# Two layers of attention and MLP on one core: VectorE's share of the exponentials gets a tile of its own, a new gate, and new numbers in the planner

## The chip, the cores and the metric

The kernel runs on one core of one Trainium2 chip. The core has five engines that run side by side: TensorE (PE in the profile) for matmuls, VectorE (DVE), ScalarE (ACT), GpSimd (POOL) and SyncE (SP), which issues the DMAs. Each engine takes its instructions in the order in which the program wrote them and waits on semaphores for the others. The metric is the time of one execution on the device in microseconds.

## What is computed

`x` is 2048 rows of 448. It goes twice through attention and a squared-ReLU MLP, with the same weights both times:

```python
x = x + _A_ref(_layernorm(x), A_wqkv, A_wo)
x = x + _B_ref(_layernorm(x), B_w1, B_b1, B_w2, B_b2)
x = x + _A_ref(_layernorm(x), A_wqkv, A_wo)
x = x + _B_ref(_layernorm(x), B_w1, B_b1, B_w2, B_b2)
```

In `_A_ref` there are 16 heads of width 28, and each head takes the softmax of a 2048 x 2048 matrix of scores. In `_B_ref` the hidden width is 1792: `h = x @ w1 + b1`, then `relu(h)` squared, then `@ w2 + b2`. The exponentials are the bulk of the elementwise work: 2 layers x 16 heads x 2048 x 2048 values, which is 2048 units of 128 x 512.

## The kernel before

**Units and groups.** The scores are cut into units of 128 keys-rows x 512 columns (one head, two blocks of 128 keys, 256 queries). `s_stream` (L746) takes three units at a time, a group: the score matmuls (L810) write three banks of a PSUM tile `sc`, of which there are two. `e_stream` (L826) then has ScalarE take the exponential of the whole group in one instruction (L835), from `sc` into a bfloat16 tile `pt`. There are 11 `pt` tiles. `p_stream` (L934) multiplies the exponentials with V (L984) and adds up `oT`.

**VectorE's units.** When `apart` (L704) says yes, the third unit of a group is not given to ScalarE: ScalarE's instruction is then 1024 columns wide, and VectorE computes the third exponential with five instructions (`a_unit` L880, `a_rest` L899). It takes the scores from PSUM and turns them into integers, `i` (L891); from the upper half of each integer it makes a power of two, `e` (L905); it multiplies a first factor into `e` (L911); it makes a second factor from the lower half, `f`, and writes it over `i` (L917); and it multiplies the two into a bfloat16 tile (L924). `f` is the lower half of `i`, so L917 writes what L911 has to have read. There are two sets of scratch tiles, `R_v`: `v_i` and `v_e`, and for most of the run a second pair that lies in a part of `K_sb` that is not in use.

**When `apart` says yes.** A set must be free, a place for the result must be free, the keys and queries must be there, the group number must be at least `LEAD` = 20, and there must be at least `STOP` = 90 units to come. Then comes a gate on VectorE's load: `pl.load(SPAN, "DVE")` is the share of the last 14 us in which VectorE was busy by the planner's reckoning. If it is above `BUSY` = 0.95 the answer is no; and if the MLP work of the layer is behind a straight line through `LINES` (`behind`, L689), the bound is `LOW` = 0.8.

**The planner.** There is no run-time scheduler. `Planner.run` (L172) simulates the engines while the program is being written: every `Op` carries an engine, a duration and what it depends on. At each step it takes, of the next operations of all streams, the one that can start first, and where two can start at the same time the one whose stream has the lower number. The order so found is the order of the instructions in each engine's queue, and nothing changes it later. For VectorE the planner lets the next operation start 0.08 us before the end of the one in front (`OVER`), and lets an operation that depends on another one of VectorE start no earlier than 0.03 us after its end. The streams' numbers are 0 for scores, 1 for ScalarE's exponentials, 2 for `p_stream`, `C_PRIO` = 1.5 for L891, `EV` = 3.5 for evictions of PSUM tiles, 4 to 4.8 for the MLP chains of the blocks (`chain`, L1118), and for the other four instructions of a VectorE unit `V_PRIO` = 7, falling to `V_LATE` = 3.6 when the unit has waited for 5.5 us and to `V_LAST` = 1.8 when it is 8 groups old.

**The rest of VectorE's work.** It evicts the projections (L572, L576, L604), the transposes (L506), the ReLU and its square (L1162, L1169), the sums into `x_sb` (L1115) and `oT` (L1007, L1009); and it takes the row moments for the layer norms: `stats` (L444) is one planner operation of 0.74 us that writes two instructions one behind the other, L449 (the moments of a row) and L450 (their mean and variance), of which the second needs the first. GpSimd makes the reciprocal root (L471, L472), and L521 applies it.

**Fill.** TensorE's score matmuls are repeated up to three times where it would sit idle, and `heat` (L1205) adds matmuls whose result nobody reads (L1220).

Of the kernel before, what the change touches and what calls it, by code (L numbers as in the profile page):

```python
# [11 lines left out]
DT = mybir.dt  # L12
# [26 lines left out]
LINES = ((280, 1312, 7.6), (1440, 2040, 6.6))  # L39
MARGIN = 2.0  # L40
LOW = 0.8
TURNS = 1
# [11 lines left out]
WINDOW = 2.8  # L54
C_PRIO = 1.5
V_PRIO = 7.0
V_LATE = 3.6
V_LAST = 1.8
V_AGE = 8
V_PAST = 3  # L60
OWN3 = 0
FIRST = 90
V_FIRST = 9.2
V_WAIT = 5.5
NEAR = 9
FAR = 15
KEEP = 3
LAG = 5
LEAD = 20
LAST = 690  # L70
BUSY = 0.95
SPAN = 14.0
NPT = 11
# [9 lines left out]
HOLD1 = 7  # L83
SOON = 0.6
NHP = 3
THIRD = 1
NL = 0
NLP = 3.8
STOP = 90
HSTOP = 0  # L90
CHUNK = 2
EV = 3.5
CUTS = (0, 10, 16)
# [124 lines left out]
def kernel(  # L218
# [225 lines left out]
    def stats(mv, t0, j, deps):  # L444
        def fn(e):
            st = sp.tile([P, 6], DT.float32, name="st")
            if mv[0] is None:
                mv[0] = sp.tile([P, 4, 2], DT.float32, name="mv")
            nc.vector.bn_stats(out=st[:, :], in_=x_sb[:, t0 + j, :])  # L449
            nc.vector.bn_aggr(out=mv[0][:, j, :], in_=st[:, :])  # L450
        o = Op("DVE", 0.74, fn, deps=deps)
        mv[1].append(o)
        return o

    def layernorm(t0, nt, deps_of, early=False, mv=None, place=None):


        if mv is None:
            mv = moments()
            for j in range(nt):  # L460
                yield stats(mv, t0, j, deps_of(j))
        ln = {}
# [23 lines left out]
        def turn(p0, own, xs):  # L486
            box = {}

            def tr(e, xs=xs):
                tp = bank(t, "tp").bitcast(DT.bfloat16).rearrange("p (c q) -> p c q", c=NDC)  # L490
                box["t"] = tp
                for k, (xn, _) in enumerate(xs):
                    for dc in range(NDC):
                        nc.tensor.transpose(out=tp[:, dc, k * P:(k + 1) * P],  # L494
                                            in_=xn[:, dc * P:(dc + 1) * P], identity=ident[:, :])
            t = Op("PE", 0.07 * NDC * len(xs), tr, deps=[x[1] for x in xs],
                   acq=pools_now(early) if early else spare(1))
            yield t

            def ev(e, p0=p0, w=len(xs) * P):  # L500
                tp = box["t"]
                dst = xnT[:, :, p0 * P:p0 * P + w]
                if e == "ACT":
                    nc.scalar.copy(out=dst, in_=tp[:, :, 0:w])
                else:
                    nc.vector.tensor_copy(out=dst, in_=tp[:, :, 0:w])  # L506
            o = Op("DVE", 0.12 + 0.3 * len(xs), ev, deps=[t], rel=t, sets=[("xT", t0 + p0)] if early else ())
            ends.append(o)
            pl.spawn(EV, iter([o, Op("DVE", 0.0, None, deps=[t], rel=own)]))

        wide = 1 if single else 2
        for p0 in range(0, nt, wide):
            js = range(p0, min(p0 + wide, nt))
            own = Op("DVE", 0.0, None, acq=R_xn)
            yield own
            xs = []
            for j in js:
                xn = xns[2 * (own.turn % 2) + j % 2]

                def norm(e, j=j, xn=xn):  # L520
                    nc.vector.tensor_scalar(out=xn[:, 0:D], in0=x_sb[:, t0 + j, :],  # L521
                                            scalar1=mv[0][:, j, 0:1], scalar2=ln[j],
                                            op0=ALU.subtract, op1=ALU.mult)
                nm = Op("DVE", 0.42, norm, deps=[rss[j]], sets=[("n", t0, j)] if early else ())
                yield nm
                xs.append((xn, nm))

            todo.append((p0, own, xs))
            if early and p0 + wide < nt:
                continue  # L530
            while todo:
                p0, own, xs = todo.pop(0)
                yield from turn(p0, own, xs)
        return xnT, own_xt, ends

    def mm_tile(subs, evac, ev_dur, deps, any_engine=False, sets=(), early=False, post=(), acq=None, alone=0):
# [25 lines left out]
        e = Op(engs_now(early) if any_engine else ("DVE",), ev_dur, lambda e: evac(e, box["t"]), deps=[last], rel=first, acq=acq, sets=sets)  # L562
        pl.spawn(EV, iter([e, *[p(e) for p in post]]))
        return e
# [14 lines left out]
    def qkv(l, t0, nt, xnT, own_xt, ends, early=False):  # L579
# [4 lines left out]
        def turned(w, dst, key, wkey, g0, r=r):  # L584
# [4 lines left out]
                 for i, g in enumerate(range(g0, g0 + r))],  # L589
                copy_to(d, q_scale if key == "Q" else None), 0.14 + 0.00109 * r * n, [*ends, *[(wkey, g) for g in range(g0, g0 + r)]], True,  # L590
                [(key, l, g, tb) for g in range(g0, g0 + r) for tb in range(t0, t0 + nt)], early and (t0 or g0 == 0))
# [97 lines left out]
    def behind(i):  # L689
# [3 lines left out]
        return done[l] < (min(i, b) - a) / (b - a) * n * per[l] - MARGIN  # L693
    pending = [0]

    def sets_of(unit):
# [7 lines left out]
    def apart(i, now, us, soon=SOON):  # L704
# [20 lines left out]
        if any(pl.tok.get(d) is None or pl.tok[d].end + LAT["DVE"] > now for d in needs(units[j])):  # L725
            return None
        if pl.load(SPAN, "DVE") > (LOW if behind(i) else BUSY):
            return None
        return j
# [96 lines left out]
    def e_stream():  # L826
        gi = 0
        while gi < len(gbuf) or s_left:
# [3 lines left out]
            def fn(e, gi=gi, n=n):  # L832
# [4 lines left out]
                if gbuf[gi].get("x") is gbuf[gi]["s"]:  # L837
                    apart_from(gi, t)
            o = gbuf[gi]["e"] = Op("ACT", n / 1200 + 0.05, fn, deps=[("s", gi)], acq=R_pt, need=n // 512,
                                   rel=gbuf[gi]["s"], sets=("e", gi))  # L840
# [25 lines left out]
    v_i = const.tile([P, 512], DT.int32, name="v_i")  # L866
    v_e = const.tile([P, 512], DT.int32, name="v_e")

    def set_of(res, l):

        k = R_v.index(res)
        two = lambda a: a.rearrange("p (a n) -> p a n", a=2)
        if k == 0:
            i, e = two(v_i[:, :]), two(v_e[:, :])
        else:
            keys = K_sb[1 - l][:, :, S - 512:S] if l == 0 else K_sb[0][:, :, 0:512]
            i, e = keys[:, 0:2, :].bitcast(DT.int32), keys[:, 2:4, :].bitcast(DT.int32)
        return i, e, two

    def a_unit(gi, x, src, unit, l):  # L880
# [3 lines left out]
        def take(e):  # L884
            pending[0] -= 1
            box["i"], box["e"], two = set_of(c.res, l)
            box["two"] = two
# [5 lines left out]
            if x is gbuf[gi]["s"]:  # L893
                apart_from(gi, t)
        c = Op("DVE", 0.69, take, deps=[("s", gi)], acq=sets_of(unit), rel=x)
        yield c
        pl.spawn(lambda now: V_LAST if e_now[1] - gi >= V_AGE or at[0] > ends_at[unit[0]] + V_PAST else V_LATE if now > c.end + V_WAIT else V_PRIO if gi > FIRST else V_FIRST, a_rest(gi, c, box, unit))

    def a_rest(gi, c, box, unit):  # L899
# [7 lines left out]
        p = Op("DVE", 0.42, power, deps=[c])  # L907
        yield p

        def first(e):  # L910
            nc.vector.scalar_tensor_tensor(out=flt("e"), in0=box["f"], scalar=root, in1=flt("e"),  # L911
                                           op0=ALU.add, op1=ALU.mult)
        g = Op("DVE", 0.68, first, deps=[p])
        yield g

        def square(e):
            nc.vector.scalar_tensor_tensor(out=flt("i"), in0=box["f"], scalar=lin, in1=box["f"],  # L917
                                           op0=ALU.add, op1=ALU.mult)
        h = Op("DVE", 0.68, square, deps=[c])
        yield h  # L920

        def close(e):
            pd = gbuf[gi]["pd"] = pd_of(o)
            nc.vector.scalar_tensor_tensor(out=box["two"](pd), in0=flt("i"), scalar=low, in1=flt("e"),  # L924
                                           op0=ALU.add, op1=ALU.mult)
        o = Op("DVE", 0.68, close, deps=[g, h], acq=lambda: pd_free(unit), rel=c, sets=("x", gi))
        gbuf[gi]["x"] = o
        yield o

    norm_done = {}  # L930
# [108 lines left out]
    def norm_stream(l, qb, g, res, oe, pair):  # L1039
# [13 lines left out]
        def rcp(e):  # L1053
            box["r"] = rp.tile([P, 2, QR], DT.float32, name="rec")[:, 0, :]
            nc.vector.reciprocal(out=box["r"][:, 0:n], in_=box["t"][:, 0:n])  # L1055
        r = Op("DVE", n * 0.0066, rcp, deps=[d], rel=d, acq=R_rec)
        yield r
# [12 lines left out]
    def norm_pair(l, qb, g, pair):  # L1070
# [15 lines left out]
        def rcp(e):  # L1086
            nc.vector.reciprocal(out=box["d"][:, :, 0:w], in_=box["d"][:, :, 0:w])
        r1 = Op("DVE", 0.33, rcp, deps=[d1])
        yield r1
# [28 lines left out]
    def chain(l, qb):  # L1118
# [10 lines left out]
        for j in range(nt):  # L1129
            a = yield from mm_tile(  # L1130
                [(0, D, [(oTn[:, g, j * P:(j + 1) * P], wo[:, g, :], *([("on", l, qb, g)] if end else [])) for g in range(G)])],
                add_to_x(t0 + j), 0.62, [*([] if end else norm_done[l, qb]), *[("wo", i) for i in range(G)]],
                post=[lambda a, j=j: stats(mv, t0, j, [a])], alone=G - 1 if end else 0)
# [18 lines left out]
        for f0 in range(0, NFC, pack):  # L1152
# [18 lines left out]
            def then(o, b=b, square=square):  # L1171
                aside = not s_left and (l, qb) == (1, len(blocks[1]) - 2)
                b["s"] = Op("ACT" if aside else "DVE", 0.5 if aside else 0.42, square, deps=[o], rel=o)
                return b["s"]
            o = yield from mm_tile(
                [(i * n, n, [(w1[:, dc, fc * P:(fc + 1) * P], xnT[:, dc, 0:n]) for dc in range(NDC)])
                 for i, fc in enumerate(fcs)],
                relu, 0.70, [*ends, ("w1",)], True, post=[then], acq=R_r)
            done[l] += w / 512
# [4 lines left out]
        for j in range(nt):  # L1184
# [3 lines left out]
            for lo, hi in halves:  # L1188
                def store(e, tb=tb, lo=lo, hi=hi):
# [5 lines left out]
                    post=[(lambda a, j=j: stats(mv, t0, j, [a])) if l == 0 else  # L1195
                          (lambda a, store=store: Op("DMA", 0.5, store, deps=[a]))])
            done[l] += 2.8
# [73 lines left out]
```

## Time and profile before

Three runs took 881.72, 882.03 and 882.49 us; the median is 882.03. The profiled execution has a span of 880.3 us, so 1.7 us lie around the span.

| | busy us | share of the span | instructions |
|---|---|---|---|
| ScalarE | 865.8 | 98% | 704 |
| of it the exponentials (L835) | 852.0 | 97% | 683 |
| TensorE | 825.4 | 94% | 12786 |
| VectorE | 795.1 | 90% | 1567 |
| GpSimd | 39.2 | 4% | 98 |

Of the 683 exponentials, 528 are 1536 columns wide and 155 are 1024 wide; VectorE has 154 units (528 x 3 + 155 x 2 + 154 = 2048). A row of the groups is to be read as: line, engine, operation, what it writes and reads, count, busy time and mean duration in ns, and the idle time of the engine just before. A row of the waits reads: who waited, for whom, us in total, how often, the longest. Instructions of one engine can overlap, so durations may add up to more than busy time.

### The profile page before, as it was taken

The page shows a single profiled execution, that of the slowest core. Times are in us where ns is not written, and L with a number is a line of the kernel's source. Part 1 is how long each engine was busy: PE and PEld are TensorE (multiplying, and loading weights), DVE is VectorE, ACT ScalarE, POOL GpSimd, SP SyncE. Part 2 cuts the span into 40 slices and gives each one's busy share as a digit, 9 for nine tenths or more (in the row PEclk, how much of TensorE's full clock was granted, in tenths as well). Part 3 has the DMA queues.
Part 4 walks back from the last instruction along what each step waited for, and adds up shares of the span by engine and source line. Part 5 has one row for each costly group of instructions (what it writes and reads, how often), then busy time and mean ns, then how long its engine had stood idle before and what let it go on. Part 6 is the DMA issues. An engine that isn't in the chain of part 4 may idle for free.

```text
span 880.3 us, 29041 instructions
## 1 busy us (share of the span) xinstructions
PE 825.4 (94%) x12786; PEld 452.0 (51%) x12786; DVE 795.1 (90%) x1567; ACT 865.8 (98%) x704; POOL 39.2 (4%) x98
## 2 busy tenths in 40 slices
PE   9999999999999999999999999899999999999998
PEld 5455554544545445455554545444545454445566
DVE  7998999999999899999989999999989899999854
ACT  8999999999999999999999999999999999999995
POOL 3100000001010000100001000000000000000000
PEclk9999999999999999999999999999999999999999
DMA  9100100000000000000000000110000000000100
GB/s 260 45 3 1 28 15 15 14 15 16 14 3 14 14 15 15 11 6 15 1 2 2 1 2 2 28 28 27 24 9 20 25 20 20 19 7 15 32 20 13
DMA packets 33914, 18.43 MB, mean 21 GB/s; under 512 B 18874, under 2 KB 33339, under 8 KB 33788
## 3 DMA queue, kind: packets, MB, share of 16 engines
q1 hardware_dynamic: 33788, 16.58, 6.8%
q8 instruction: 100, 1.64, 0.7%
q14 instruction: 26, 0.21, 0.1%
HBM read 14.26 MB, written 2.07 MB: 19 GB/s over the span
## 4 chain that ended last, share of the span: by engine, by line
ACT 77%; issue 12%; PE 10%; DVE 0%; ACTq 0%
ACT pt L835 77%; PE mt L554 4%; PE sc L810 3%; PE oT L984 2%; PE sc L554 1%; PE mt L330 1%; PE tp L494 0%; PE mt L1220 0%; DVE rec L1055 0%; PE den L1049 0%; DVE xnT L506 0%; ACT r L1160 0%; DVE oTn L1060 0%; DVE x_sb L1115 0%; DVE b2w L312 0%
## 5 line engine op out<-in xcount | busy, mean ns | idle before, releaser
L835 ACT ACTIVATE pt<-sc 128x1536 bf16<-128x1536 f32 (+1 forms) x683 | 852.0, 1527 | 1.2 <-PE sc L810 1.2
L810 PE MATMUL sc<-Q_sb,K_sb 32*128 32x256 bf16 (+1 forms) x5806 | 321.1, 265 | 45.3 <-ACT pt L835 39.9
L810 PEld LDWEIGHTS <-K_sb 32*128 32x128 bf16 x5806 | 151.2, 92 | 223.6 <-issue 191.5
L984 PE MATMUL oT<-pt,V_sb 128*32 128x256 bf16 (+1 forms) x4034 | 151.9, 268 | 0.0
L554 PE MATMUL mt<-xnT,w 128*128 128x256 bf16 (+1 forms) x912 | 119.8, 270 | 1.8 <-DVE xnT L506 0.6
L984 PEld LDWEIGHTS <-V_sb 128*32 128x32 bf16 x4352 | 91.0, 96 | 46.1 <-issue 43.1
L554 PEld LDWEIGHTS <-w 128*128 128x128 bf16 x952 | 78.7, 98 | 36.9 <-issue 28.9
L1162 DVE TENSOR_SCALAR r<-mt 128x512 bf16<-128x512 f32 x106 | 72.3, 682 | 8.2 <-PE mt L554 7.3
L554 PE MATMUL mt<-w,V_sb 128*128 128x448 bf16 (+2 forms) x288 | 67.9, 346 | 0.0
L891 DVE TENSOR_SCALAR v_i<-sc 128x512 int32<-128x512 f32 x87 | 59.5, 684 | 9.0 <-PE sc L810 8.6
L917 DVE SCALAR_TENSOR_TENSOR v_i<-v_i 128x512 f32<-128x512 uint16 x87 | 59.4, 683 | 1.3
L911 DVE SCALAR_TENSOR_TENSOR v_e<-v_i,v_e 128x512 f32<-128x512 uint16 x87 | 59.4, 683 | 0.8
L891 DVE TENSOR_SCALAR K_sb<-sc 128x512 int32<-128x512 f32 x67 | 45.8, 683 | 9.1 <-PE sc L810 9.0
L917 DVE SCALAR_TENSOR_TENSOR K_sb<-K_sb 128x512 f32<-128x512 uint16 x67 | 46.0, 687 | 1.3
L471 POOL TENSOR_TENSOR ve<-mv,eps_t 128x2 f32<-128x2 f32 (+1 forms) x34 | 9.5, 279 | 827.2 <-DVE mv L450 827.2
L911 DVE SCALAR_TENSOR_TENSOR K_sb<-K_sb 128x512 f32<-128x512 uint16 x67 | 45.8, 684 | 0.4
L1220 PE MATMUL mt<-xn,ident 128*128 128x448 bf16 x127 | 44.3, 356 | 1.6 <-DVE xn L521 0.6
L1115 DVE TENSOR_TENSOR x_sb<-x_sb,mt 128x448 bf16<-128x448 bf16 (+2 forms) x63 | 37.8, 601 | 7.5 <-PE mt L554 7.3
L449 DVE BATCH_NORM_STATS2 st<-x_sb 128x6 f32<-128x448 bf16 x64 | 39.7, 620 | 1.1 <-DMA x_sb<-in_A_x_dram 0.6
L554 PEld LDWEIGHTS <-V_sb 128*128 128x128 bf16 x302 | 24.9, 97 | 24.6 <-issue 10.1
L905 DVE TENSOR_SCALAR v_e<-v_i 128x512 int32<-128x512 int16 x87 | 36.4, 418 | 0.4
L984 PE MATMUL oT<-V_sb,V_sb 128*32 128x256 bf16 (+1 forms) x182 | 32.4, 273 | 0.0
(102 smaller groups left out, 792.1 us busy)
## 6 DMA issues: line engine op xcount, KB each, us to landing
rec<-scr SPq DMA_DIRECT2D x56, 128.0 KB
x_sb<-in_A_x_dram SPq DMA_DIRECT2D x8, 224.0 KB
out_dram<-x_sb SPq DMA_DIRECT2D x15, 112.0 KB
w<-in_B_w_dram SPq DMA_DIRECT2D x1, 1568.0 KB
w<-in_B_w_dram SPq DMA_DIRECT2D x1, 1344.0 KB
dn<-oT_sb SPq DMA_DIRECT2D x56, 4.0 KB
V_sb<-in_A_wqkv_dram SPq DMA_DIRECT2D x4, 168.0 KB
scr<-dn SPq DMA_DIRECT2D x28, 8.0 KB
```

The source lines that it names most:

```text
L449: nc.vector.bn_stats(out=st[:, :], in_=x_sb[:, t0 + j, :])
L554: nc.tensor.matmul(box["t"][:, c0:c0 + n], lhsT=lhsT() if callable(lhsT) else lhsT, rhs=rhs, start=a, stop=b)
L810: nc.tensor.matmul(dst[k][:, i * nt * P:(i + 1) * nt * P], lhsT=K_sb[l][rows, g, (kb + i) * P:(kb + i + 1) * P], rhs=Q_sb[rows, g, t0 * P: ...
L835: t = nc.scalar.activation(out=pt[:, 0:n], in_=gbuf[gi]["sc"][:, 0:n], func=AF.Exp, scale=float(np.log(2.0)) * 2.0 ** -FRAC)
L891: t = nc.vector.tensor_scalar(out=box["i"], in0=two(src), scalar1=EXP_BIAS, scalar2=EXP_LOW, op0=ALU.add, op1=ALU.max)
L905: nc.vector.tensor_scalar(out=box["e"], in0=box["n"], scalar1=2.0 ** 22, scalar2=EXP_BASE, op0=ALU.mult, op1=ALU.add)
L911: nc.vector.scalar_tensor_tensor(out=flt("e"), in0=box["f"], scalar=root, in1=flt("e"), op0=ALU.add, op1=ALU.mult)
L917: nc.vector.scalar_tensor_tensor(out=flt("i"), in0=box["f"], scalar=lin, in1=box["f"], op0=ALU.add, op1=ALU.mult)
L984: nc.tensor.matmul(box["t"][DHP * hh:DHP * hh + DHP, 0:n], lhsT=V_sb[l][:, kb + i, 4 * g + hh, :], rhs=p[:, c0:c0 + n], start=begin and kb ...
L1115: nc.vector.tensor_tensor(out=x_sb[:, tb, lo:hi], in0=x_sb[:, tb, lo:hi], in1=t[:, 0:hi - lo], op=ALU.add)
L1162: nc.vector.tensor_scalar(out=r[:, 0:w], in0=t[:, 0:w], scalar1=0.0, scalar2=None, op0=ALU.max)
L1220: nc.tensor.matmul(t[:, 0:D], lhsT=ident[:, :], rhs=xns[0][:, 0:D], start=True, stop=True)
```

## The change

Five things are changed together.

1. A scratch tile `v_h` is added. For the set `v_i`/`v_e` the second factor (L917) goes into `v_h` and not over `i`; it depends on L891 alone and is put in front of L911. For the set in `K_sb` the second factor still goes over `i`; it now depends on L911 in the planner's eyes too.
2. `stats` becomes two planner operations, 0.62 us and 0.182 us, so that another instruction may come between them.
3. Many durations in the planner are replaced; an exponential of n columns is n/1200 + 0.066 us where it was n/1200 + 0.05.
4. `apart` has a new gate: VectorE's open work, that is how far its clock is ahead plus what is left of the units begun (2.74 us for one just begun), must not be above `TB` = 4.8 us, or above `TB2` = 1.2 us when the MLP is behind. The load gate stays, over 8 us and not 14, with `BUSY` = 1.1 and `LOW` = 0.9.
5. The streams' numbers and other constants are changed.

```diff
-MARGIN = 2.0
-LOW = 0.8
+MARGIN = 1.5
+LOW = 0.9
...
-C_PRIO = 1.5
-V_PRIO = 7.0
-V_LATE = 3.6
-V_LAST = 1.8
+C_PRIO = 2.3
+V_PRIO = 8.5
+V_LATE = 5
+V_LAST = 2.7
 V_AGE = 8
-V_PAST = 3
+V_PAST = 4
 OWN3 = 0
-FIRST = 90
-V_FIRST = 9.2
-V_WAIT = 5.5
-NEAR = 9
+FIRST = 110
+V_FIRST = 7
+V_WAIT = 3.5
+NEAR = 10
 FAR = 15
-KEEP = 3
-LAG = 5
-LEAD = 20
+KEEP = 2
+LAG = 6
+LEAD = 10
 LAST = 690
-BUSY = 0.95
-SPAN = 14.0
+BUSY = 1.1
+TB = 4.8
+TB2 = 1.2
+SPAN = 8
...
-EV = 3.5
+EV = 2.9
...
     def stats(mv, t0, j, deps):
-        def fn(e):
-            st = sp.tile([P, 6], DT.float32, name="st")
+        box = {}
+
+        def take(e):
+            box["st"] = sp.tile([P, 6], DT.float32, name="st")
+            nc.vector.bn_stats(out=box["st"][:, :], in_=x_sb[:, t0 + j, :])
+
+        def merge(e):
             if mv[0] is None:
                 mv[0] = sp.tile([P, 4, 2], DT.float32, name="mv")
-            nc.vector.bn_stats(out=st[:, :], in_=x_sb[:, t0 + j, :])
-            nc.vector.bn_aggr(out=mv[0][:, j, :], in_=st[:, :])
-        o = Op("DVE", 0.74, fn, deps=deps)
+            nc.vector.bn_aggr(out=mv[0][:, j, :], in_=box["st"][:, :])
+        s = Op("DVE", 0.62, take, deps=deps)
+        o = Op("DVE", 0.182, merge, deps=[s])
         mv[1].append(o)
-        return o
+        return s, o
...
+        if max(0.0, pl.clock["DVE"] - now) + left[0] > (TB2 if behind(i) else TB):
             return None
         return j
...
-            o = gbuf[gi]["e"] = Op("ACT", n / 1200 + 0.05, fn, deps=[("s", gi)], acq=R_pt, need=n // 512,
+            o = gbuf[gi]["e"] = Op("ACT", n / 1200 + 0.066, fn, deps=[("s", gi)], acq=R_pt, need=n // 512,
...
+    v_h = const.tile([P, 512], DT.float32, name="v_h")
...
         c = Op("DVE", 0.69, take, deps=[("s", gi)], acq=sets_of(unit), rel=x)
+        left[0] += 2.74
         yield c
+        left[0] -= 0.6
...
-        g = Op("DVE", 0.68, first, deps=[p])
-        yield g
+        g = Op("DVE", 0.684, first, deps=[p])
 
         def square(e):
-            nc.vector.scalar_tensor_tensor(out=flt("i"), in0=box["f"], scalar=lin, in1=box["f"],
+            nc.vector.scalar_tensor_tensor(out=box["h"], in0=box["f"], scalar=lin, in1=box["f"],
                                            op0=ALU.add, op1=ALU.mult)
-        h = Op("DVE", 0.68, square, deps=[c])
-        yield h
+        alone = c.res is R_v[0]
+        h = Op("DVE", 0.684, square, deps=[c] if alone else [c, g])
+        for k in (h, g) if alone else (g, h):
+            yield k
+            left[0] -= 0.6
...
-        r = Op("DVE", n * 0.0066, rcp, deps=[d], rel=d, acq=R_rec)
+        r = Op("DVE", 0.16 + n * 0.00623, rcp, deps=[d], rel=d, acq=R_rec)
```

The other durations that change: the eviction of a transpose from 0.12 + 0.3 to 0.15 + 0.265 us per block, the norm (L521) from 0.42 to 0.39, the projections' evictions from 0.698 to 0.683 at 512 columns, the ReLU from 0.70 to 0.685, the sum into `x_sb` from 0.62 to 0.61, the small reciprocal from 0.33 to 0.25. `SOON` and `NLP` change too, but nothing reads them with `OWN3` = 0, `THIRD` = 1 and `NL` = 0.

More of the change, by code (lines that the diff above doesn't have):

```diff
@@ L83 @@
 HOLD1 = 7
-SOON = 0.6
+SOON = 0.8
 NHP = 3
@@ L87 @@
 NL = 0
-NLP = 3.8
+NLP = 4.6
 STOP = 90
@@ L460, in layernorm @@
             for j in range(nt):
-                yield stats(mv, t0, j, deps_of(j))
+                yield from stats(mv, t0, j, deps_of(j))
         ln = {}
@@ L506, in ev @@
                     nc.vector.tensor_copy(out=dst, in_=tp[:, :, 0:w])
-            o = Op("DVE", 0.12 + 0.3 * len(xs), ev, deps=[t], rel=t, sets=[("xT", t0 + p0)] if early else ())
+            o = Op("DVE", 0.15 + 0.265 * len(xs), ev, deps=[t], rel=t, sets=[("xT", t0 + p0)] if early else ())
             ends.append(o)
@@ L523, in norm @@
                                             op0=ALU.subtract, op1=ALU.mult)
-                nm = Op("DVE", 0.42, norm, deps=[rss[j]], sets=[("n", t0, j)] if early else ())
+                nm = Op("DVE", 0.39, norm, deps=[rss[j]], sets=[("n", t0, j)] if early else ())
                 yield nm
@@ L562, in mm_tile @@
         e = Op(engs_now(early) if any_engine else ("DVE",), ev_dur, lambda e: evac(e, box["t"]), deps=[last], rel=first, acq=acq, sets=sets)
-        pl.spawn(EV, iter([e, *[p(e) for p in post]]))
+        pl.spawn(EV, iter([e, *[o for p in post for o in p(e)]]))
         return e
@@ L589, in turned @@
                  for i, g in enumerate(range(g0, g0 + r))],
-                copy_to(d, q_scale if key == "Q" else None), 0.14 + 0.00109 * r * n, [*ends, *[(wkey, g) for g in range(g0, g0 + r)]], True,
+                copy_to(d, q_scale if key == "Q" else None), 0.145 + 0.00105 * r * n, [*ends, *[(wkey, g) for g in range(g0, g0 + r)]], True,
                 [(key, l, g, tb) for g in range(g0, g0 + r) for tb in range(t0, t0 + nt)], early and (t0 or g0 == 0))
@@ L694 @@
     pending = [0]
+    left = [0.0]
     def sets_of(unit):
@@ L727, in apart @@
         if pl.load(SPAN, "DVE") > (LOW if behind(i) else BUSY):
+            return None
+        if max(0.0, pl.clock["DVE"] - now) + left[0] > (TB2 if behind(i) else TB):
             return None
@@ L873, in set_of @@
         if k == 0:
-            i, e = two(v_i[:, :]), two(v_e[:, :])
+            i, e, h = two(v_i[:, :]), two(v_e[:, :]), two(v_h[:, :])
         else:
@@ L877, in set_of @@
             i, e = keys[:, 0:2, :].bitcast(DT.int32), keys[:, 2:4, :].bitcast(DT.int32)
-        return i, e, two
+            h = i.bitcast(DT.float32)
+        return i, e, h, two
     def a_unit(gi, x, src, unit, l):
@@ L885, in take @@
             pending[0] -= 1
-            box["i"], box["e"], two = set_of(c.res, l)
+            box["i"], box["e"], box["h"], two = set_of(c.res, l)
             box["two"] = two
@@ L908, in a_rest @@
         yield p
+        left[0] -= 0.34
         def first(e):
@@ L912, in first @@
                                            op0=ALU.add, op1=ALU.mult)
-        g = Op("DVE", 0.68, first, deps=[p])
-        yield g
+        g = Op("DVE", 0.684, first, deps=[p])
         def square(e):
-            nc.vector.scalar_tensor_tensor(out=flt("i"), in0=box["f"], scalar=lin, in1=box["f"],
+            nc.vector.scalar_tensor_tensor(out=box["h"], in0=box["f"], scalar=lin, in1=box["f"],
                                            op0=ALU.add, op1=ALU.mult)
-        h = Op("DVE", 0.68, square, deps=[c])
-        yield h
+        alone = c.res is R_v[0]
[3 more added lines that the diff above has]
+            left[0] -= 0.6
         def close(e):
             pd = gbuf[gi]["pd"] = pd_of(o)
-            nc.vector.scalar_tensor_tensor(out=box["two"](pd), in0=flt("i"), scalar=low, in1=flt("e"),
+            nc.vector.scalar_tensor_tensor(out=box["two"](pd), in0=box["h"], scalar=low, in1=flt("e"),
                                            op0=ALU.add, op1=ALU.mult)
-        o = Op("DVE", 0.68, close, deps=[g, h], acq=lambda: pd_free(unit), rel=c, sets=("x", gi))
+        o = Op("DVE", 0.683, close, deps=[g, h], acq=lambda: pd_free(unit), rel=c, sets=("x", gi))
         gbuf[gi]["x"] = o
         yield o
+        left[0] -= 0.6
     norm_done = {}
@@ L1087, in rcp @@
             nc.vector.reciprocal(out=box["d"][:, :, 0:w], in_=box["d"][:, :, 0:w])
-        r1 = Op("DVE", 0.33, rcp, deps=[d1])
+        r1 = Op("DVE", 0.25, rcp, deps=[d1])
         yield r1
@@ L1131, in chain @@
                 [(0, D, [(oTn[:, g, j * P:(j + 1) * P], wo[:, g, :], *([("on", l, qb, g)] if end else [])) for g in range(G)])],
-                add_to_x(t0 + j), 0.62, [*([] if end else norm_done[l, qb]), *[("wo", i) for i in range(G)]],
+                add_to_x(t0 + j), 0.61, [*([] if end else norm_done[l, qb]), *[("wo", i) for i in range(G)]],
                 post=[lambda a, j=j: stats(mv, t0, j, [a])], alone=G - 1 if end else 0)
@@ L1173, in then @@
                 b["s"] = Op("ACT" if aside else "DVE", 0.5 if aside else 0.42, square, deps=[o], rel=o)
-                return b["s"]
+                return [b["s"]]
             o = yield from mm_tile(
@@ L1177, in chain @@
                  for i, fc in enumerate(fcs)],
-                relu, 0.70, [*ends, ("w1",)], True, post=[then], acq=R_r)
+                relu, 0.685, [*ends, ("w1",)], True, post=[then], acq=R_r)
             done[l] += w / 512
@@ L1195, in chain @@
                     post=[(lambda a, j=j: stats(mv, t0, j, [a])) if l == 0 else
-                          (lambda a, store=store: Op("DMA", 0.5, store, deps=[a]))])
+                          (lambda a, store=store: [Op("DMA", 0.5, store, deps=[a])])])
             done[l] += 2.8
```

## The prediction

> **What bounds the kernel.** I read the page's first part and its chain of waits, then ScalarE's waits and TensorE's, then ScalarE's groups by shape.
>
> ```profile
> span 880.3 us, 29041 instructions
> ...
> PE 825.4 (94%) x12786; PEld 452.0 (51%) x12786; DVE 795.1 (90%) x1567; ACT 865.8 (98%) x704; POOL 39.2 (4%) x98
> ...
> PEclk9999999999999999999999999999999999999999
> ...
> ACT 77%; issue 12%; PE 10%; DVE 0%; ACTq 0%
> ```
> ```profile
> ACT pt L835 <- PE sc L810: 1.2, 3, 0.6
> ```
> ```profile
> PE sc L810 <- ACT pt L835: 39.9, 109, 0.7
> ```
> ```profile
> L835 ACT ACTIVATE pt<-sc 128x1536 bf16<-128x1536 f32 x528 | 743.4, 1620 | 1.2 <-PE sc L810 1.2
> L835 ACT ACTIVATE pt<-sc 128x1024 bf16<-128x1024 f32 x155 | 176.4, 1210 | 0.0
> ```
>
> ScalarE runs exponentials from 11.1 us to 864.1 us. In those 853 us it waits for scores three times, 1.2 us in all, while the score matmuls wait for ScalarE 109 times. So time is the number of columns that ScalarE is given, plus 11.1 us in front and 16.2 us behind. In ScalarE's timeline the next exponential starts 1.331 us after a wide one and 0.905 us after a narrow one (medians; neighbours overlap, so the means of 1620 and 1210 ns are too long for spacing, though their difference, 0.41, is near). **Each unit that moves to VectorE takes 0.426 us off the end.** Nothing else in the middle of the run counts, unless it makes ScalarE wait. The question is how many more than 154 units VectorE gets, and whether it delivers them in time.
>
> **How much room VectorE has.** In stretches of 40 us (columns: window, length, PE, PEld, DVE, ACT, POOL busy with counts, clock, DMA share, GB/s):
>
> ```profile
> 240.00:280.00 40.00, 37.47 (x575) 19.40 (x576) 37.26 (x72) 40.00 (x34) 2.75 (x6) 1.00 0.04 10
> ...
> 680.00:720.00 40.00, 37.78 (x560) 19.78 (x554) 35.88 (x72) 40.00 (x33) 1.30 (x2) 1.00 0.07 21
> ...
> 760.00:800.00 40.00, 36.91 (x564) 19.17 (x558) 38.30 (x75) 40.00 (x33) 0.89 (x2) 1.00 0.08 22
> ```
>
> VectorE is busy for 37.3 us of 40 on average over the 18 stretches from 80 to 800 us (35.88 the least, 38.38 the most), and idle for 58 us of the 800 between 40 and 840. A unit is five instructions: 684 + 418 + 683 + 683 + 682 = 3150 ns by the groups' means. The timeline shows what they occupy:
>
> ```profile
> 467.01 0.62 DVE L449 BATCH_NORM_STATS2 st<-x_sb 128x6 f32<-128x448 bf16 x1
> 467.66 0.18 DVE L450 BATCH_NORM_AGGREGATE mv<-st 128x2 f32<-128x6 f32 x1
> 467.76 0.66 DVE L917 SCALAR_TENSOR_TENSOR v_i<-v_i 128x512 f32<-128x512 uint16 x1
> ...
> 469.65 0.69 DVE L911 SCALAR_TENSOR_TENSOR K_sb<-K_sb 128x512 f32<-128x512 uint16 x1
> 470.37 0.69 DVE L917 SCALAR_TENSOR_TENSOR K_sb<-K_sb 128x512 f32<-128x512 uint16 x1
> 470.98 0.68 DVE L891 TENSOR_SCALAR v_i<-sc 128x512 int32<-128x512 f32 x1
> ```
>
> L917 ends at 471.06 and the unrelated L891 has begun at 470.98: 0.08 us of overlap. L450 needs L449 and begins 0.03 us after its end; L917 overwrites what L911 reads and does the same. Counted over the timeline, unrelated neighbours overlap by 82 ns, dependent ones stand 34 ns apart: a dependent neighbour costs 116 ns. A unit whose instructions are spread among others therefore takes 3150 - 5 x 82 = 2740 ns.
>
> **Part 1 and 2, the stalls.** There are 272 such stalls in the trace, 31.6 us: 73 from L911 to L917 (37 in the set that gets `v_h`, 36 in `K_sb`), 64 from L449 to L450, 32 from L905 to L911, 25 from L917 to L924, the rest elsewhere. The planner doesn't know the first two kinds: it has no dependence between L911 and L917, and `stats` is one operation. With the change it sees all of them, and since it takes whatever starts first, any ready operation goes in between. I take three in four as filled between 40 and 840 us.
> - `stats`: 46 of the 64 lie there; 0.75 x 46 x 0.116 = 4.0 us.
> - Set with `v_h`: the 37 go, and so do the 22 of its stalls between L905 and L911, which now has L917 in front of it; but L924 now needs its immediate predecessor in the queue more often. I net 37 + 22 - 20 = 39, or 4.5 us.
> - Set in `K_sb`: 0.75 x 36 x 0.116 = 3.1 us.
>
> Sum 11.6 us of VectorE. Ends: 0 if nothing is ready to go between, 16 us if all are filled.
>
> Here a rule speaks against the change. The Trainium skill, "VectorE: DVE Perf Modes", section "The DRAIN you can't avoid", says that after every VectorE instruction the pipe empties before the next starts, that chaining without semaphores doesn't skip it[...]. By that rule the order is indifferent, `v_h` and the split save 0 us, and 3.7 units (1.6 us of the end) of the sum below fall away. The rows above disagree: 82 ns of overlap for one pair, 34 ns of gap for the other, in the same stretch. I go by the rows.
>
> **Part 4, the gate.** I compared each group's start with VectorE's load over the 14 us before it. Between 120-400 and 440-800 us, 155 groups had a free set and gave no unit; for 102 of them the load was 0.95 or more. So the cap of 0.95 is what refuses most. Afterwards `BUSY` = 1.1 refuses nothing and the 4.8 us of open work allow a second unit whenever the first is under way (2.74 left plus up to 2.06 of clock). While the MLP is behind, `LOW` = 0.9 over 8 us and 1.2 us of open work hold a unit back until the last is nearly closed: looser in load, stricter in count. How often it is behind no view shows. Bounds on what this fills: 0 (the strict side wins) to 40 us (VectorE idle for only 18 of the 800). The nearest row is the best stretches that this same work has reached, 38.3 of 40; I take that for all: 18 x (38.3 - 37.3) = 18 us, and 1.7 us from 40-80 (36.6 now). Sum 20 us.
>
> **Units.** One more unit costs VectorE 2.74 us, and the shorter run takes 0.426 x 0.94 = 0.4 us of VectorE time away: 3.14. (11.6 + 20) / 3.14 = 10. `LEAD` = 10 lets the first unit come ten groups, some 13 us, earlier than 37 us; but VectorE is busy for 18.4 of the 20 us from 20 to 40, so I take 1 unit (ends 0 and 4). Eleven units: 154 -> 165, **-4.7 us**.
>
> **Part 3 and 5, at nothing.** Durations: the old exponential of the model is 1.33 us for wide, the trace has 1.331 as median and 852.0/683 over all fits 1.344; with the new 1.346 the plan no longer has ScalarE too fast by 683 x 0.016 = 11 us over the run, which loosens VectorE in the plan. I don't count it again beside the gate. No instruction, wait or DMA is added; SP's queue keeps its DMAs, and `rec` was waited for 1.0 us only. What is queued behind a VectorE instruction that waits is the rest of VectorE, so lower priority for the units (8.5 for 7) makes MLP evictions earlier, if anything. The cover of all this is ScalarE's unbroken row. If it breaks, each us of score delay is a us of the end. In front, ScalarE idles 3.75 us before 40 us; unchanged. Behind the last exponential is the chain of the last blocks, 16.2 us, which `EV` below the normalisation's 3 can reorder: bounds -1.5 to +1.5, taken as 0.
>
> **Sum.** 880.3 - 4.7 = 875.6 us of span; with the 1.7 us around it **877.3 us**, against the median of 882.03.
>
> **Rivals.**
> - *VectorE filled to the brim.* For it: with the cap gone, something is always open, and 16 us of stalls and 40 us of idle time are there: 56 / 3.14 = 18 units, -7.6 us, 874.4 us. Against it: 21 waits of L891 for scores (17.6 us) and 7.8 us for GpSimd's root are gaps that more open units fill only in part.
> - *The gate is no wider.* The MLP is behind most of the time, 1.2 us of open work stops what the load allowed, and only the stalls' 11.6 us turn into units, 3 or 4: 880.4 us, within 0.2% of 882.03 (1.8 us, about what a measurement of this kernel can tell from no change).
> - *Late units stop TensorE.* This is the other side. A unit lives 5.9 us now (median, L891's start to L924's end); with numbers of 8.5, 5 and 2.7 for 7, 3.6 and 1.8 and a fuller VectorE it closes later. TensorE is in order: an `oT` matmul that waits for L924 holds the scores behind it. Their cover is thin: the last score matmul ends 0.22 us (median) before its exponential starts. Today its matmuls wait 0.4 us for L891 and its weight loads 0.4 us, once, for L924. If each of 165 units costs ScalarE 0.04 us on average (one in ten stopping it for 0.4 us), that is 6.6 us: 883.9 us. It decides from 4.7 / 165 = 0.028 us a unit.
>
> **Chances.** Forecast 0.50 (its own range 875.3 to 879.5), brim 0.22, gate no wider 0.12, late units 0.16. Faster takes the first two and a share of the third, 0.74; same 0.11; slower 0.15. The range runs from 872.0 (brim, with the tail's 1.5 us) to 883.5, into the late units' case.
>
> **What would show it.** Count of L891: 165 right, 158 the narrow gate, 172 the brim. L835 at 1024 columns one more than that. VectorE's stretches at 38.3 of 40. L450 no longer 0.03 us behind L449 but with another line between, and L917 in front of L911 for `v_h`. ScalarE's wait for scores still about 1 us; 5 us or more, with TensorE waiting for L924 or L891, would be the slower rival. I am wrong if units rise and time doesn't fall by 0.426 us each, or if the stretch after the last exponential moves by more than 1.5 us.

## The result, and the profile after

The changed kernel takes 876.67 us (median of four executions; 876.35 to 877.08) against 882.11 us for the kernel before, which ran a fourth time here: a ratio of 0.9937 with a 95% interval of 0.9923 to 0.9951, so 0.6% faster. The profiled execution has a span of 875.0 us. The forecast was 877.3 us.

The page's first part and the head of its chain of waits, for the changed kernel:

```profile
span 875.0 us, 29070 instructions
...
PE 823.4 (94%) x12774; PEld 448.9 (51%) x12774; DVE 824.6 (94%) x1657; ACT 858.6 (98%) x704; POOL 44.5 (5%) x98
...
ACT 54%; DVE 22%; PE 14%; issue 9%; DMA 1%; SPq 0%; POOL 0%; DVEq 0%; ACTq 0%
```

VectorE is 29.5 us busier in a shorter run. The chain now runs through VectorE for 22% of the span, where it had 0%; ScalarE, at 54%, is still the larger part. ScalarE's exponentials by shape, and then its waits for scores; the third view has TensorE's waits for the instruction with which VectorE takes over a unit (L891 before, L903 after), first before, then after:

```profile
L845 ACT ACTIVATE pt<-sc 128x1536 bf16<-128x1536 f32 x510 | 726.2, 1588 | 2.7 <-PE sc L820 2.4
L845 ACT ACTIVATE pt<-sc 128x1024 bf16<-128x1024 f32 x173 | 198.9, 1159 | 0.3 <-PE sc L820 0.3
```
```profile
ACT pt L845 <- PE sc L820: 2.7, 6, 1.1
```
```profile
PE sc L810 <- DVE K_sb L891: 0.4, 1, 0.4
...
PE sc L820 <- DVE K_sb L903: 1.4, 4, 0.5
...
PE sc L820 <- DVE v_i L903: 1.1, 3, 0.5
```

Narrow exponentials went from 155 to 173, so VectorE has **172 units, 18 more**. The wait for scores rose from 1.2 to 2.7 us. In the 40 us stretches (columns as before):

```profile
240.00:280.00 40.00, 38.86 (x576) 20.38 (x567) 39.82 (x81) 40.00 (x34) 2.37 (x6) 1.00 0.04 10
...
400.00:440.00 40.00, 38.16 (x564) 20.47 (x558) 34.01 (x63) 40.00 (x32) 2.43 (x6) 1.00 0.01 2
...
680.00:720.00 40.00, 38.19 (x558) 19.73 (x556) 39.87 (x80) 40.00 (x34) 1.30 (x2) 1.00 0.08 22
...
760.00:800.00 40.00, 38.46 (x583) 20.25 (x583) 39.39 (x78) 40.00 (x34) 1.43 (x2) 1.00 0.07 21
```

Where both sets of scratch tiles may be used, VectorE is busy for 39.4 to 39.9 of 40 us. Where one set is allowed it stays lower (34.0 from 400 to 440). Over the 18 stretches from 80 to 800 us the mean is 39.05, where it was 37.3. Between 40 and 840 us its idle time fell from 58 to 26 us. VectorE's timeline shows why it packs so well:

```profile
466.26 0.42 DVE L919 TENSOR_SCALAR v_e<-v_i 128x512 int32<-128x512 int16 x1
466.60 0.69 DVE L931 SCALAR_TENSOR_TENSOR v_h<-v_i 128x512 f32<-128x512 uint16 x1
...
468.66 0.62 DVE L451 BATCH_NORM_STATS2 st<-x_sb 128x6 f32<-128x448 bf16 x1
469.19 0.68 DVE L926 SCALAR_TENSOR_TENSOR v_e<-v_i,v_e 128x512 f32<-128x512 uint16 x1
469.79 0.18 DVE L456 BATCH_NORM_AGGREGATE mv<-st 128x2 f32<-128x6 f32 x1
...
470.79 0.69 DVE L926 SCALAR_TENSOR_TENSOR K_sb<-K_sb 128x512 f32<-128x512 uint16 x1
471.51 0.69 DVE L931 SCALAR_TENSOR_TENSOR K_sb<-K_sb 128x512 f32<-128x512 uint16 x1
```

The instruction that writes `v_h` starts 0.08 us before the one that writes `v_e` ends, and another line stands between the two halves of a moment (L451 and L456). The last two lines are a stall that is left, in the set that has no third tile. Counted over the timeline, stalls fell from 272 to 102.

**The account.** The span can be added up from ScalarE's starts: the first exponential, 1.331 us after each wide one and 0.905 us after each narrow one, what each start is late beyond that, the last exponential itself (1.3 to 1.5 us), and the stretch after it ends. All from the traces, in us:

| run | units | first | late starts, sum | of it 500-600 us | after the last | span |
|---|---|---|---|---|---|---|
| before | 154 | 11.1 | 9.6 | 1.0 | 16.2 | 880.3 |
| changed | 172 | 10.7 | 12.0 | 0.9 | 16.5 | 875.0 |
| e1 | 168 | 10.7 | 22.7 | 12.9 | 21.2 | 892.3 |
| e2 | 154 | 10.8 | 11.2 | 1.0 | 24.3 | 889.8 |
| e3 | 173 | 10.6 | 26.7 | 6.8 | 19.5 | 892.3 |
| e4 | 158 | 10.7 | 14.3 | 1.4 | 16.8 | 883.4 |
| e5 | 172 | 10.9 | 12.3 | 1.2 | 19.5 | 878.6 |
| e6 | 170 | 11.1 | 19.7 | 5.1 | 23.8 | 891.3 |
| e7 | 174 | 11.0 | 26.8 | 11.2 | 24.1 | 896.8 |
| e8 | 173 | 10.8 | 33.3 | 15.7 | 21.2 | 900.7 |

From before to changed: 18 x 0.426 = 7.7 us less work, 0.4 us earlier start, 2.4 us more late starts, 0.3 us more behind: 5.4 us, and the spans differ by 5.3. Most of the lateness is invisible in the view of waits: a wide exponential is recorded with 1.59 us on average and the next starts after 1.331, so a start that is 0.1 us late shows no idle time.

In the column of late starts, 1.1 of the 2.4 us more lie before 24.4 us, where the first VectorE unit starts. The six runs in which a moment is two operations have 1.9 us there, the four in which it is one have 0.8 to 0.9.

Two things besides the order are in these spans. The granted clock of TensorE was 0.5 for a while in some traces: for 6.83 us in e2 and e6 and for 3.41 us in e8 behind the last exponential, and at the stops described below for 6.83 us in e7 and 3.41 us in e3 and e8; e7 has another 6.83 us behind the last exponential, e3 another 3.41 us at 31 us. Half of that time, 3.4 us each and 6.8 us in e7, is an estimate of the most that it can have cost. And e1's trace is of its fastest execution.

### The profile page after: what moved, and what is told of

It reads as the page before. It is cut to its first block, busy times and chain, and to the rows that moved or that the text cites. A ratio compares the mean times of both kernels' runs of the same rounds, so it can differ in the third digit from the quotient of the medians.

```text
span 875.0 us, 29070 instructions
## 1 busy us (share of the span) xinstructions
PE 823.4 (94%) x12774; PEld 448.9 (51%) x12774; DVE 824.6 (94%) x1657; ACT 858.6 (98%) x704; POOL 44.5 (5%) x98
## 4 chain that ended last, share of the span: by engine, by line
ACT 54%; DVE 22%; PE 14%; issue 9%; DMA 1%; SPq 0%; POOL 0%; DVEq 0%; ACTq 0%
ACT pt L845 53%; PE mt L561 6%; PE sc L820 4%; DVE V_sb L941 2%; PE oT L1002 2%; DVE r L1180 2%; DVE v_i L903 2%; DVE K_sb L926 2%; DVE v_e L926 1%; DVE K_sb L903 1%; DVE st L451 1%; DVE x_sb L1133 1%; DVE v_h L931 1%; DVE K_sb L931 1%; PE sc L561 1%
## 5 line engine op out<-in xcount | busy, mean ns | idle before, releaser
L820 PEld LDWEIGHTS <-K_sb 32*128 32x128 bf16 x5780 | 147.5, 92 | 216.9 <-issue 179.7
L903 DVE TENSOR_SCALAR v_i<-sc 128x512 int32<-128x512 f32 x97 | 66.3, 684 | 2.3 <-PE sc L820 1.7
L931 DVE SCALAR_TENSOR_TENSOR v_h<-v_i 128x512 f32<-128x512 uint16 x97 | 66.2, 682 | 0.0
L926 DVE SCALAR_TENSOR_TENSOR v_e<-v_i,v_e 128x512 f32<-128x512 uint16 x97 | 66.1, 681 | 0.0
L903 DVE TENSOR_SCALAR K_sb<-sc 128x512 int32<-128x512 f32 x75 | 51.2, 682 | 3.4 <-PE sc L820 2.9
L478 POOL TENSOR_TENSOR ve<-mv,eps_t 128x2 f32<-128x2 f32 (+1 forms) x34 | 11.1, 326 | 816.8 <-DVE mv L456 816.8
L926 DVE SCALAR_TENSOR_TENSOR K_sb<-K_sb 128x512 f32<-128x512 uint16 x75 | 51.3, 685 | 1.0
L931 DVE SCALAR_TENSOR_TENSOR K_sb<-K_sb 128x512 f32<-128x512 uint16 x75 | 51.1, 681 | 0.5
L1238 PE MATMUL mt<-xn,ident 128*128 128x448 bf16 x141 | 47.6, 356 | 1.0 <-DVE V_sb L611 0.3
L1133 DVE TENSOR_TENSOR x_sb<-x_sb,mt 128x448 bf16<-128x448 bf16 (+1 forms) x64 | 38.6, 605 | 5.3 <-PE mt L561 5.2
L919 DVE TENSOR_SCALAR v_e<-v_i 128x512 int32<-128x512 int16 x97 | 40.5, 418 | 0.3
L451 DVE BATCH_NORM_STATS2 st<-x_sb 128x6 f32<-128x448 bf16 x64 | 39.1, 615 | 0.8 <-DMA x_sb<-in_A_x_dram 0.7
L1002 PE MATMUL oT<-V_sb,V_sb 128*32 128x256 bf16 (+1 forms) x200 | 37.6, 276 | 0.3 <-DVE V_sb L941 0.2
```

The source lines that it names most:

```text
L451: nc.vector.bn_stats(out=box["st"][:, :], in_=x_sb[:, t0 + j, :])
L820: nc.tensor.matmul(dst[k][:, i * nt * P:(i + 1) * nt * P], lhsT=K_sb[l][rows, g, (kb + i) * P:(kb + i + 1) * P], rhs=Q_sb[rows, g, t0 * P: ...
L903: t = nc.vector.tensor_scalar(out=box["i"], in0=two(src), scalar1=EXP_BIAS, scalar2=EXP_LOW, op0=ALU.add, op1=ALU.max)
L919: nc.vector.tensor_scalar(out=box["e"], in0=box["n"], scalar1=2.0 ** 22, scalar2=EXP_BASE, op0=ALU.mult, op1=ALU.add)
L931: nc.vector.scalar_tensor_tensor(out=box["h"], in0=box["f"], scalar=lin, in1=box["f"], op0=ALU.add, op1=ALU.mult)
L1002: nc.tensor.matmul(box["t"][DHP * hh:DHP * hh + DHP, 0:n], lhsT=V_sb[l][:, kb + i, 4 * g + hh, :], rhs=p[:, c0:c0 + n], start=begin and kb ...
```

## The experiments

Each run takes parts of the change out or puts them in, with a new plan each time, since the planner writes the order anew.

**e1: the gate alone.** The kernel before with these lines, and the bookkeeping of `left` that they need (cut to what matters):

```diff
-LOW = 0.8
+LOW = 0.9
...
-BUSY = 0.95
-SPAN = 14.0
+BUSY = 1.1
+TB = 4.8
+TB2 = 1.2
+SPAN = 8
...
+        if max(0.0, pl.clock["DVE"] - now) + left[0] > (TB2 if behind(i) else TB):
+            return None
```

> The kernel before with the new gate alone (BUSY 1.1, LOW 0.9, SPAN 8, TB 4.8, TB2 1.2); old tile, old moments, old durations, old stream numbers. Theory A (the gate brings the units): 168 units on VectorE, 14 more than before; 14 x 0.426 = 6.0 us less work for ScalarE, less some 2 to 4 us of late starts of ScalarE because the plan doesn't know the stalls: 878 to 880 us. Rival B (stalls removed bring the units, the gate only shifts them): no gain, 881 to 883 us. Rival C (a fuller VectorE makes ScalarE late by as much as the units bring): 882 us or more, with ScalarE's late starts up by 6 us.

Measured: 897.07 us, ratio 1.016 (1.0138 to 1.0182). The units came, 168 of them, and the time went the other way: by 12 us in the trace, which is of the execution of 894.1 us with a clock of 1.00, and by 15 us in the median. The other three executions took 896.2 to 898.2 us with a mean clock of 0.992 to 0.996. ScalarE's timeline around the change of layers:

```profile
529.29 10.25 ACT L840 ACTIVATE pt<-sc 128x1536 bf16<-128x1536 f32 x8
551.48 5.97 ACT L840 ACTIVATE pt<-sc 128x1024 bf16<-128x1024 f32 x5 [11.94 <-PE sc L815]
```

It stands still for 11.9 us. The chain of waits there, start and length of each piece:

```profile
544.70 0.63 DVE x_sb L1128
...
546.55 0.70 POOL rstd L474
...
548.47 0.70 DVE xnT L508
...
549.22 1.05 PE mt L556 x8
...
550.29 0.70 DVE K_sb L578
...
551.04 0.42 PE sc L815 x7
```

Layer 2's scores begin earlier, with the keys of the first 1280 rows (`CUTS` in the kernel; by e1's plan at 434 us). The group that stops is the first that needs the keys of the last 256 rows, and these rows' MLP, norm and K projection end at 550.99. "The change of layers" stands for this date here. All three rivals fail in part: theory A had the units right, but the place of the loss is neither the stalls nor late single units. With the gate as the only change, the new order puts the MLP of these rows past a date on which everything waits for it. Another 5 us went behind the last exponential.

**e2: tile and moments alone.** The kernel before with parts 1 and 2 of the change (the diff of `stats` and of `square`).

> The kernel before with the second factor in its own tile, the new order of the two factors and the moments as two steps; old gate, durations and stream numbers. The prediction's step: 11.6 us of stalls become 3 or 4 units, 880.4 us. Theory A (the gate alone decides how many units, and it doesn't see stalls): 154 units, time within 1 us of before (881 to 882.5), VectorE's busy time down by some 9 us and its idle time up.

Measured: 891.53 us, 1.010 (1.0085 to 1.0115). Units 154, as theory A said; the time is 9 to 11 us above what either theory gave. The stalls fell from 272 to 142 and VectorE's busy time by 10 us with the same work:

```profile
PE 829.3 (93%) x12781; PEld 456.5 (51%) x12781; DVE 785.1 (88%) x1566; ACT 866.2 (97%) x705; POOL 44.3 (5%) x98
```

None of it became time, and 8.1 us were lost behind the last exponential. ScalarE's timeline there, first in this run, then in the changed kernel:

```profile
849.33 16.16 ACT L845 ACTIVATE pt<-sc 128x1536 bf16<-128x1536 f32 x12
874.30 0.60 ACT L1178 ACTIVATE r<-mt 128x512 bf16<-128x512 f32 x1 [8.81 <-PE mt L561]
```
```profile
843.82 14.76 ACT L845 ACTIVATE pt<-sc 128x1536 bf16<-128x1536 f32 x11
859.58 0.60 ACT L1178 ACTIVATE r<-sc 128x512 bf16<-128x512 f32 x1 [1.00 <-PE sc L561]
```

In e2 an attention sum of the last blocks, its moments and its transposes still had to come before the first ReLU; in the changed kernel the first came after 1.0 us. Most of this is the order that the planner chose: from the end of the last exponential to the end of its last operation, its own plan has 17.0 us for the kernel before and 22.8 for e2, 5.8 of the 8.1 us. The rest is not separated; the clock was 0.5 from 869.87 to 876.70 us.

**e3, e7 and e8: tile and moments taken out,** both and one at a time, from the changed kernel. The edits put the old lines of parts 1 and 2 back, with the changed kernel's durations for the factors.

> The changed kernel with the moments in one step again and the second factor over i again: 173 units. Theory A (the stalls' removal is what lets VectorE keep to the plan): some 140 stalls of 0.116 us are back, 16 us on a VectorE that is nearly full, so ScalarE starts late more often: 878 to 881 us. Rival B (VectorE has slack enough): 876 us, as the changed kernel.

> The changed kernel with the moments as one step: 174 units. 64 stalls of 0.116 us are back, 46 of them where VectorE is full, and each moment takes 0.09 us longer than its 0.74 in the plan. If the stalls count one by one: 2 units more, -0.9 us, and 5 us of VectorE back of which ScalarE sees a part: 876 to 881 us. If what counts is that the plan is wrong about the chip, the half of the 16 us that the run without tile and moments lost: 883 to 886 us.

> The changed kernel with the second factor over i again, behind the first, with no dependence of the one on the other in the plan: 173 units. 78 pairs stand one behind the other, 9 us of stalls that the plan doesn't know. If they count one by one: 877 to 881 us; if the larger share of the loss without tile and moments is theirs: 884 to 890 us.

Measured: e3 892.83 us, 1.0119 (1.0103 to 1.0135); e7 898.24 us, 1.0176 (1.0161 to 1.0191); e8 902.06 us, 1.0219 (1.0204 to 1.0235). All the expected ranges were too low, and taking out one part costs more than taking out both. So the loss can't be a price per stall. The account shows where it lies: 6 to 15 us more late starts at the change of layers, 4 to 9 us more elsewhere in the row, and 3 to 8 us more behind the last exponential. The stop in e7:

```profile
534.60 8.49 ACT L840 ACTIVATE pt<-sc 128x1536 bf16<-128x1536 f32 x7
553.38 7.31 ACT L840 ACTIVATE pt<-sc 128x1024 bf16<-128x1024 f32 x6 [10.30 <-PE sc L815]
```

**e4: the old gate in the changed kernel.**

```diff
-LOW = 0.9
+LOW = 0.8
...
-BUSY = 1.1
-TB = 4.8
-TB2 = 1.2
-SPAN = 8
+BUSY = 0.95
+TB = 1000
+TB2 = 1000
+SPAN = 14.0
```

With 1000 us the bound on open work refuses nothing.

> The changed kernel with the old gate (BUSY 0.95, LOW 0.8 over 14 us, no bound on open work): 158 units. Theory A (units make the time, 0.426 us each, less late starts): 4 more units than before, 880 to 880.7 us. Rival (the new stream numbers and durations make the time by fewer late starts): 878 us or less with late starts of ScalarE below those of before.

Measured: 885.4 us, 1.0032 (1.0019 to 1.0045); units 158. The change of layers and the end are in order (1.4 and 16.8 us), so here units can be priced: against the changed kernel 14 x 0.426 = 6.0 us, 2.3 us more late starts, 0.3 us behind: 8.6 us, and the medians differ by 8.7. Why late starts are more with fewer units no run shows. Theory A's 880 to 880.7 us was too low because of them: they are 4.7 us above those of the kernel before. The rival, that numbers and durations make the time, falls: without the new gate they, tile and moments make it 3.2 us worse than before.

**e5: the old stream numbers and other constants,** all the rest changed.

> The changed kernel with the old stream numbers and other constants (MARGIN, C_PRIO, V_PRIO, V_LATE, V_LAST, V_PAST, FIRST, V_FIRST, V_WAIT, NEAR, KEEP, LAG, LEAD, EV); new gate, tile, moments and durations: 172 units, as many as the changed kernel. Theory A (the stream numbers keep the MLP ahead of VectorE's units, so that layer 2's keys are there in time): ScalarE stands still at the layer change near 545 us for 4 us or more and the stretch after the last exponential is longer than 16.5 us: 882 us or more. Rival B (the new durations do that): 876 to 878 us.

Measured: 880.56 us, 0.9979 (0.9969 to 0.9988). Same 172 units, late starts within 0.3 us of the changed kernel, no stop at the change of layers. The time lies between the two expected ranges. Theory A is wrong at the change of layers and right at the end: 3.0 us more behind the last exponential, where ScalarE waits 4.69 us for the first ReLU:

```profile
863.81 0.60 ACT L1178 ACTIVATE r<-mt 128x512 bf16<-128x512 f32 x1 [4.69 <-PE mt L561]
```

The numbers are worth 3.6 us between the traces (3.9 between the medians), and most of it is the order of the last blocks.

**e6: the old durations in the plan,** all the rest changed.

> The changed kernel with the old durations in the plan: 170 units. Theory B of the run before (the durations keep the plan true, so the order fits the chip): ScalarE's late starts grow and the layer change stalls: 881 us or more. Theory A: two units fewer, 0.9 us, 877 to 878.5 us.

Measured: 893.25 us, 1.0117 (1.01 to 1.0134): 170 units, 3.7 us of late start at 143.8 us, 4.1 us at 547.8, 23.8 us behind the last exponential. The time and the two stops are as theory B forecast. Its reason does not fit: the stops are not the chip falling behind the plan, they stand in the plan itself, 3.8 us at 137 us and 4.4 us at 539 us. Theory A's two units fewer came as well.

**Plan and chip.** The planner knows when it expects the last exponential to end. Its own figure, written out by each kernel's planner, beside the end in the trace:

```
                            plan    chip   chip - plan
before                      855.5   864.1   8.6
e1 gate alone               862.6   871.0   8.5
e2 tile and moments         857.5   865.5   8.0
e6 old durations            860.2   867.6   7.4
e3 without tile, moments    865.3   872.9   7.6
e7 moments in one           869.6   872.7   3.1
e8 second factor over i     876.2   879.5   3.3
e4 old gate                 866.4   866.6   0.2
e5 old numbers              859.1   859.1   0.0
changed                     859.4   858.6  -0.8
```

Here the order is the same on both sides, so a difference is what the plan doesn't know. With old durations it is 7 to 9 us, and e2, which knows the stalls, still has 8.0. With new durations it is 3.1 us where the moments are one operation, 3.3 us where the second factor goes over `i`, and 7.6 us with both. Not all of that is stalls: 1.4 us of it in e7, 1.4 in e8 and 2.8 in e3 arise in the stretches in which the clock was 0.5. With tile, moments and new durations, plan and chip agree within 1 us. Most of the loss of e7 and e8 is in their plans: their last exponentials are planned 10.2 and 16.8 us later than the changed kernel's, e3's 5.9 us later. It also settles where the stops come from: e1's plan has a gap of 13.0 us in ScalarE's row that ends at 546 us, e8's one of 13.0 at 553, e7's one of 9.0 at 550. The greedy choice of one ready operation after another made them; on the chip they are 12.3, 14.5 and 10.5 us of late start.

What wasn't tried: the changed kernel's own order with the stalls put back by hand, which would price the stalls without a new plan on the chip; and why a small edit sends the greedy choice past the date at one time and not at another stays open.

## Why the prediction was right, and where it was not

- **What bounds.** Right: with 0.426 us a unit the account closes within 0.2 us. But the prediction read 1.2 us of waits as all that ScalarE loses, and the account has 9.6 us of late starts before. By the prediction's own sign (time must fall by 0.426 us for each unit) it would have been wrong: 18 units brought 5.4 us, 0.30 each.
- **"Part 1 and 2, the stalls."** The size was about right: 11.6 us between 40 and 840 us were forecast, and e2 shows 130 stalls fewer over the whole run, 15.1 us at 0.116, with VectorE 10 us less busy. The step from there to 3.7 units was wrong: 154 units in e2. Units are given by the plan, and 117 of the 130 stalls are of the two kinds that the old plan didn't know, so their removal showed it no room; that this is the reason is argued, not tested by itself. What the parts buy, together with the new durations, is a plan that agrees with the chip within 1 us.
- **The rule weighed against the rows.** The rows were right: the same 154 units with 130 stalls fewer take 10 us less of VectorE. That order is indifferent was too much to read from the Trainium skill, "VectorE: DVE Perf Modes": the section "The DRAIN you can't avoid" itself makes an exception, that a next instruction which is not held starts earlier. The 82 ns of overlap agree with that exception; no run here tests what holds an instruction.
- **"Part 4, the gate."** The mis-sized term. 38.3 of 40 us was taken as the level reached; it was 39.4 to 39.9 where two sets may be used, and 39.05 over all 18 stretches. Alone it brings 14 units (e1), its removal takes 14 (e4); forecast were 20 / 3.14 = 6.
- **"`LEAD`, I take 1 unit."** The first unit starts at 24.4 us and not 37, and two lie before 40 us where there was one: right.
- **"Part 3 and 5, at nothing."** The net effect in the whole was small, but nothing it was not: old numbers cost 3.6 us of span (e5), old durations 16.3 us (e6), in which 6.83 us at half clock are contained. The prediction's cover was ScalarE's unbroken row; it overlooked the two dates on which that row depends on the MLP, the change of layers and the end.
- **"Taken as 0" behind the last exponential.** 16.2 to 16.5 us, inside the bounds of 1.5; that another order can make it 8 us longer (e2) was outside of them.
- **The rivals.** The count was that of the brim, 172. Late units came too, but small: of the 2.4 us more late starts at most 1.3 us can be theirs, since 1.1 us lie before the first unit; TensorE's scores waited 2.5 us for L903 where they had waited 0.4 us for L891. So the forecast's number was met by luck, by errors of opposite sign: 7 units too few (3.0 us) and an earlier first exponential (0.4 us) on one side, and 2.7 us of late starts and end that weren't in the sum on the other.

## What to carry to other kernels

Where a program's order is made by a planner, a change of its costs is a new order, and taking one part out measures that new order as much as the part: keep an account of work, late starts and ends, and compare the plan with the chip before pricing a part. Stalls between dependent instructions must be visible to whoever orders them: then most were filled here, 272 became 102, though filling them alone brought no time (e2). And a fuller helper engine must be held against dates further on, such as a change of layers, not only against the next instruction.

## What was not expected of the hardware

TensorE's granted clock fell to 0.5 in the middle of some runs. In e2, in stretches of 10 us (PE busy, with count, is the first column behind the length; the clock is the third from the end):

```profile
860.00:870.00 10.00, 7.54 (x169) 3.98 (x157) 5.46 (x12) 5.49 (x5) 0.75 (x2) 0.99 0.04 13
870.00:880.00 10.00, 8.63 (x108) 8.47 (x109) 3.57 (x11) 3.02 (x5) 0.75 (x2) 0.67 0.01 2
```

Looked at more closely, PE is busy for 1.24 us of the 3.41 us up to 869.87, and for the 6.83 us after that the clock is 0.5: the last blocks' transposes and MLP matmuls run in it. The changed kernel has 8.8 and 9.4 of 10 us busy from 850 to 870 us and keeps 1.00. Over 520 to 560 us, around their stops, e3 shows 0.96 and e7 and e8 0.91. e1's trace keeps 1.00 through a stop of 11.9 us, with 1.57 us of 3.41 busy from 545.80; its other executions had a mean clock of 0.992 to 0.996, so the same program does not always keep it. What decides no run shows. A lead, not shown: of the late starts over 30 ns after 20 us, those whose scores stood right behind a fill matmul (L1220, now L1238) add up to 2.0 us before and 3.0 us after.
